# Decoded input weights of the first dense layer: kept in six SBUF slots instead of a round trip through DRAM

## The chip, the cores and the metric

The kernel runs on one core of one Trainium2 chip. The metric is the device time of one launch in microseconds (us). Three timed runs of the kernel before gave 885.88, 887.46 and 888.39 us; their median, 887.46 us, is the time that the change is measured against. The engines are called PE (TensorE, matrix products), ACT (ScalarE), DVE (VectorE), POOL (GpSimd) and SP (SyncE, which here issues every DMA). SBUF is the on-chip working memory, DRAM the memory off the core.

## The reference

Batch B = 4, sequence S = 448, 12 heads of 64, so a model width of 768. Three stages follow each other, each reading what the one before wrote:

```
attention:  scores = 0.125 * q k^T ; mix the heads with w_pre ; softmax ; mix the heads with w_post ; times v
layer one:  h = gelu_tanh(x @ w_in)           # w_in is 768 x 1024
            u, v = h[:, :512], h[:, 512:]
            v = layernorm(v) * g_ln ;  v = w_sg @ v + b_sg
            x = x + (u * v) @ w_out           # w_out is 512 x 768
layer two:  theta = x @ w_theta               # w_theta is 768 x 768
            y = w_tok_r @ (x * cos(theta)) + w_tok_i @ (x * sin(theta))
            u = x + y ;  out = u + relu(u @ w_ch)
```

The weights of the two layers are handed over as 64-bit floats. The chip turns each into a pair of 32-bit parts, a high one and a low one ("decoding"), and a product is computed as three: high by high, high by low, low by high.

## The kernel before

One program runs the three stages one after another. The order of the instructions on each engine is the order in which the Python code emits them; an engine works through its own list strictly in that order, and waits are put in where a tile is written, read or its memory used again.

**Attention** is a software pipeline over 92 steps r, each a pair of blocks of query rows. In a step SP issues the relayout of the scores of step r+4 (`blk<-s`), PE mixes the heads with w_pre for r+2 (`psB`), DVE takes the row maximum (`nmx`), ACT the exponential (`e`), POOL scales w_post (`wr`), PE mixes the heads again (`psC`), ACT and DVE write the result in two parts (`ah`, `al`), and PE multiplies by v (`psD`). Scores of a later tile (`psA`, drained by ACT into `s`) run between. The finished rows go to DRAM as `xT`.

**The decoding of w_in beside attention.** Eighteen jobs of 128 x 256 values are spread over the attention steps: all six row blocks of the right half of w_in (columns 512 to 1023, the v half), and the first three of the left half (KE = 3, the u half). A job (`decode`, L563) loads 256 KB into `draw`, lets ACT and DVE build the value, and then ACT writes the high part into a tile `dh` (`high`, L602), DVE forms the remainder, and POOL writes the low part into the same tile (`low`, L613). `dh` has one buffer there. Last, SP stores `dh` into the DRAM scratch `win_d` (`store`, L618), 256 KB. So each `dh` can be written again only after the store of the one before has landed.

**The change-over to layer one.** The last attention steps and the first units of layer one are interleaved by a small table of keys (`tail` in `moe1`): at key -7 layer one's pools are opened in the memory that early attention tiles have left, and SP issues, for k = 0 to 5, two loads of `xraw` (a 448-column and a 64-column piece of `xT`) and then `load_win(k, 1)`, which brings 512 KB of decoded w_in back from `win_d` into SBUF (`load_pair`, L647). At keys 1 to 3 follow three more, `load_win(k, 0)`. ACT and DVE split each `xraw` in two parts (`x`, L547 and L550). The unit `v_chunk` multiplies 128 rows of x by the v half: for each k three products, 18 in all (`ps<-win,x`, L554). Four v_chunks are placed into attention's tail; `psD` groups of attention stand between them. The six jobs for the rest of the u half (k = 3 to 5) are decoded there too, straight into tiles of the `win` pool. Then four `u_half` units follow, and the rest of the layer.

**Layer two** needs w_theta, which layer one decodes into the DRAM scratch `wth_d`. After layer one's last u_half the `win` pool is closed and a pool `th` opened over it; twelve loads `load_wth(k, half)` (L647) fill it, placed after the units that follow.

Of the kernel before, what the change touches and what calls it, by code (L numbers as in the profile page):

```python
# [6 lines left out]
F32 = mybir.dt.float32  # L7
F32R = mybir.dt.float32r
# [10 lines left out]
DM = H * D  # L19
# [453 lines left out]
DFF = 1024  # L473
HF = DFF // 2
KD, KF = DM // 128, HF // 128
# [7 lines left out]
KE = 3  # L483
# [7 lines left out]
class Dense:  # L491


    def __init__(self, tc, nc, io, xT, x2T, outT):
        self.tc, self.nc, self.io = tc, nc, io
        self.xT, self.x2T, self.outT = xT, x2T, outT
        self.pools, self.psum = {}, None
        self.units, self.before, self.after, self.at = [], {}, {}, 0
        self.jobs, self.job_at = [], 0
        self.raw_bufs, self.mid_bufs, self.out_bufs = 1, 1, 1  # L500
        self.const = {}


    def unit(self, fn, *a):
# [50 lines left out]

    def scratch(self, dram):
        t = lambda name, r, c: dram.tile([2, r, c], F32, name=name)
        self.win_d = t("win_d", DM, DFF)
        self.wth_d = t("wth_d", DM, DM)
        self.wtok_d = t("wtok_d", 2 * S, S)  # L560
        self.wch_d = t("wch_d", 128 * KC, DM)

    def decode(self, src, n, dst, tiles=None):  # L563

# [86 lines left out]
def moe1(d, left, right):  # L651

    tc, nc, io = d.tc, d.nc, d.io
    win_es, tail_es, tail_ps = ExitStack(), ExitStack(), ExitStack()
    win, wsg, wout, xt, uT, vraw, mv, vn, mixed, gt, res = ({} for _ in range(11))
    small = {}

    def start():
        d.open("c", 1, right, "right")
        d.open("x", 1, right, "right")  # L660
        d.open("win", 1, win_es, "right")
        for name, bufs in (("st", 4), ("v", 4), ("s", 2), ("dec", 1)):
            d.open(name, bufs, tail_es, "right")
        d.open_psum(2, tail_ps, "right")
        d.raw_bufs, d.mid_bufs, d.out_bufs = 3, 4, 4
        c = d.pools["c"]
        for name in ("eps", "hpi"):
            d.const[name] = c.tile([128, 1], F32, name=name)
        d.const["sin"] = c.tile([128, 1], F32, name="sin")
        d.const["ident"] = c.tile([128, 128], F32, name="ident")  # L670
        pair = lambda pool, n, tag: [d.pools[pool].tile([128, n], F32R, tag=f"{tag}_{i}", name=tag) for i in range(2)]
        for k in range(KE, KD):
            def tiles(k=k):
                win[k, 0] = pair("win", HF, f"win{k}_0")
                return win[k, 0]
            d.jobs += d.decode_tiles(io["w_in"], slice(128 * k, 128 * k + 128), 0, HF, tiles)
        d.jobs += [None]
        for k in range(KF):
            def tiles(k=k):
                wout[k] = pair("w", DM, f"wout{k}")  # L680
                return wout[k]
            d.jobs += d.decode_tiles(io["w_out"], slice(128 * k, 128 * k + 128), 0, DM, tiles)
        d.jobs += (d.decode_all(io["w_theta"], 0, DM, d.wth_d)
                   + d.decode_all(io["w_tok"], 0, S, d.wtok_d)
                   + d.decode_all(io["w_ch"], 0, DM, d.wch_d, 128 * KC))
# [18 lines left out]
    def rest2():  # L704
        tail_es.close()
        for name, bufs in (("st", 4), ("s", 2), ("v", 4), ("g", 1)):
            d.open(name, bufs, left)

    def load_win(k, half):
        win[k, half] = d.load_pair(d.pools["win"], d.win_d, slice(128 * k, 128 * k + 128),  # L710
                                   slice(HF * half, HF * half + HF), f"win{k}_{half}")

    def load_wsg(c):
        raw = d.stage(S, "wsgraw")
# [151 lines left out]
    for b in range(B + 1):  # L866
# [13 lines left out]
        if b < B:  # L880
            g0[b] = len(d.units)
            for f in range(KF):
                i = U(gate, b, f)
# [8 lines left out]
    for b in range(B):  # L892
# [4 lines left out]
        for c in range(nv):  # L897
# [3 lines left out]
            i = o0[b - 1][0] + late_u + c  # L901
            d.post(i, norm, b, c)
            d.post(i, norm_split, b, c)
        if b + 1 < B:
            i = u0[b] + KF
# [25 lines left out]
    def at(s, fn, *a):  # L931
        tail.setdefault(s, []).append(lambda: fn(*a))
    at(-7, start)
    for k in range(KD):
        at(-7, load_x, 0, k, "st" if k < 4 else "v")
        at(-7, load_win, k, 1)
        at(-4 + k // 2, split_x, 0, k)
    at(-3, consts)
    for k in range(KE):
        at(1 + k, load_win, k, 0)  # L940
    for key in (-4, -3, -2, -2, -1, -1, 0, 1, 2, 3, 4):
        at(key, d.tick)
    for c in range(4):
# [7 lines left out]
def moe2(d, left, win_es, last_u, m1_left):  # L951
    tc, nc, io = d.tc, d.nc, d.io
    wth, wch, wtok, z, x2, st, ut, res = ({} for _ in range(8))
    th_es = ExitStack()

    def start():
        win_es.close()
        d.open("th", 1, th_es, "right")
        d.open("xp", 2, th_es, "right")

    def load_wth(k, half):
        wth[k, half] = d.load_pair(d.pools["th"], d.wth_d, slice(128 * k, 128 * k + 128),
                                   slice(384 * half, 384 * half + 384), f"wth{k}_{half}")

    def rest():
        while d.job_at < len(d.jobs) + LAGS[0][1]:
# [183 lines left out]
    first = len(d.units)  # L1150

    d.post(last_u, start)
    for k in range(KD):
        for half in range(2):
            d.post(last_u + 1 + k, load_wth, k, half)
# [36 lines left out]
    for j, kh in enumerate(words):  # L1192
        i = tok0 - 1 + (3 * j + 1) // 2
# [21 lines left out]
def build(tc, nc, io, out):  # L1215
    with tc.manual_schedule(), ExitStack() as top:
        dram = top.enter_context(tc.tile_pool(name="scratch", bufs=1, space=bass.MemoryType.DRAM))
        xT = dram.tile([DM, B * S], F32, name="xT")
        x2T = dram.tile([DM, B * S], F32, name="x2T")
        d = Dense(tc, nc, io, xT, x2T, out)  # L1220
        d.scratch(dram)
        right, left1, left2 = ExitStack(), ExitStack(), ExitStack()
        tail, win_es, last_u, end = moe1(d, left1, right)
        th_es = moe2(d, left2, win_es, last_u, left1)
        for i in range(4):
            tail.setdefault(-2 + 2 * i, []).append(d.step)
        jobs = d.decode_all(io["w_in"], HF, DFF, d.win_d)
        jobs += d.decode_all(io["w_in"], 0, HF, d.win_d, 128 * KE)
        attention(tc, nc, io, xT, B, jobs, tail)
        while d.at < len(d.units):  # L1230
            d.step()
        th_es.close()
        right.close()
        left2.close()


# [72 lines left out]
```

## Time and profile before

| | us |
|---|---|
| timed runs, median of three | 887.46 |
| the profiled execution | 892.93 |
| its span (first to last instruction) | 891.2 |
| PE busy in the span | 854.0 (96%) |
| attention, until layer one's first product | 0 to 367 |
| change-over with attention's last products | 367 to 387 |
| layer one and layer two | 387 to 891 |

Every duration in this document comes from one profiled execution of 892.93 us, 5.47 us above the median of the timed runs. A busy share is to be read by stage: PE is busy almost without a gap in the two layers, and in attention and the change-over it waits now and then. The rows in the section before the prediction show the waits that the change touches.

### The profile page before, as it was taken

The page shows a single profiled execution, that of the slowest core. Times are in us where ns is not written, and L with a number is a line of the kernel's source. Part 1 is how long each engine was busy: PE and PEld are TensorE (multiplying, and loading weights), DVE is VectorE, ACT ScalarE, POOL GpSimd, SP SyncE. Part 2 cuts the span into 40 slices and gives each one's busy share as a digit, 9 for nine tenths or more (in the row PEclk, how much of TensorE's full clock was granted, in tenths as well). Part 3 has the DMA queues.
Part 4 walks back from the last instruction along what each step waited for, and adds up shares of the span by engine and source line. Part 5 has one row for each costly group of instructions (what it writes and reads, how often), then busy time and mean ns, then how long its engine had stood idle before and what let it go on. Part 6 is the DMA issues. An engine that isn't in the chain of part 4 may idle for free.

```text
span 891.2 us, 29399 instructions
## 1 busy us (share of the span) xinstructions
PE 854.0 (96%) x12008; PEld 673.9 (76%) x12008; DVE 660.7 (74%) x1471; ACT 535.3 (60%) x1202; POOL 253.9 (28%) x453
## 2 busy tenths in 40 slices
PE   8899999999998999799999999998999999999998
PEld 2456556565665566589898989898989999999997
DVE  3887888788888888579999998969886358338221
ACT  5888789878897887466665767427535136016010
POOL 0272254225422642000000000016607228406421
PEclk9999999999999999899999999999999999999999
DMA  6567656675676545873385857997620311300301
GB/s 203 193 210 220 212 176 213 207 230 175 217 229 201 186 168 141 270 239 98 111 280 172 279 182 234 294 348 248 212 92 29 114 34 39 114 22 7 105 20 63
DMA packets 116343, 151.15 MB, mean 170 GB/s; under 512 B 26224, under 2 KB 100208, under 8 KB 116208
## 3 DMA queue, kind: packets, MB, share of 16 engines
q1 hardware_dynamic: 116208, 149.26, 52.8%
q8 instruction: 95, 1.56, 0.8%
q14 instruction: 40, 0.33, 0.1%
HBM read 78.38 MB, written 32.31 MB: 124 GB/s over the span
## 4 chain that ended last, share of the span: by engine, by line
PE 67%; DVE 9%; DMA 8%; ACT 6%; POOL 5%; issue 4%; SPq 1%; ACTq 0%; POOLq 0%; DVEq 0%
PE ps L554 46%; PE psC L302 6%; PE psB L244 5%; PE psA L219 4%; PE psD L354 4%; ACT e L258 2%; POOL vl L197 2%; ACT s L225 2%; DVE nmx L250 1%; DMA win_d<-dh 1%; POOL vraw L188 1%; DMA blk<-s 1%; POOL wr L280 1%; DMA xres<-xT 1%; ACT ah L325 1%
## 5 line engine op out<-in xcount | busy, mean ns | idle before, releaser
L258 ACT ACTIVATE e<-psB,nmx 128x448 f32<-128x448 f32 x180 | 113.1, 637 | 32.8 <-DVE nmx L250 31.6
L331 DVE SCALAR_TENSOR_TENSOR al<-psC,ah 128x480 f16<-128x480 f32 x180 | 116.3, 647 | 9.7 <-ACT ah L325 8.8
L250 DVE TENSOR_REDUCE nmx<-psB 128x1 f32<-128x448 f32 x180 | 103.9, 618 | 16.2 <-PE psB L244 13.9
L302 PE MATMUL psC<-wr,e 64*64 64x60 f32 x5632 | 106.4, 222 | 4.3 <-issue 1.9
L550 POOL TENSOR_TENSOR x2s<-x,x2s 128x384 fp32r<-128x384 f32 x28 | 28.8, 1049 | 284.8 <-ACT x2s L547 284.8
L244 PE MATMUL psB<-blk,kpre 64*64 64x448 f32 x720 | 104.0, 546 | 4.8 <-ACT e L258 3.9
L302 PEld LDWEIGHTS psC<-wr,e 64*64 64x64 f32 x5632 | 93.7, 135 | 17.0 <-POOL wr L280 7.5
L554 PE MATMUL ps<-wtok,z 128*128 128x448 f32 x504 | 104.8, 368 | 0.0
L219 PE MATMUL psA<-k,q 64*64 64x448 f32 (+2 forms) x768 | 96.5, 551 | 7.8 <-ACT s L225 5.6
L554 PEld LDWEIGHTS ps<-wtok,z 128*128 128x128 f32 x504 | 94.6, 188 | 9.5
L354 PEld LDWEIGHTS <-vh 128*64 128x64 f16 x1536 | 57.5, 112 | 58.0 <-issue 57.8
L325 ACT ACTIVATE ah<-psC 128x480 f16<-128x480 f32 x180 | 93.7, 581 | 10.3 <-PE psC L302 10.2
L554 PE MATMUL ps<-wth,x2s 128*128 128x384 f32 x504 | 93.0, 338 | 3.2 <-POOL x2s L550 2.1
L225 ACT ACTIVATE s<-psA 124x896 f32<-124x896 f32 (+1 forms) x90 | 84.2, 936 | 12.3 <-PE psA L219 7.6
L554 PEld LDWEIGHTS ps<-wth,x2s 128*128 128x128 f32 x504 | 87.1, 188 | 4.9 <-POOL x2s L550 3.0
L554 PE MATMUL ps<-u,wch 128*128 128x448 f32 x432 | 89.9, 368 | 0.0
L554 PEld LDWEIGHTS ps<-u,wch 128*128 128x128 f32 x432 | 81.1, 188 | 8.1
L550 POOL TENSOR_TENSOR z<-zz,z 128x384 fp32r<-128x384 f32 x56 | 64.4, 1170 | 55.7 <-ACT z L547 55.6
L244 PEld LDWEIGHTS psB<-blk,kpre 64*64 64x64 f32 x720 | 37.6, 132 | 50.0 <-ACT e L258 23.8
L547 ACT ACTIVATE u<-xres 128x448 fp32r<-128x448 f32 x24 | 13.8, 577 | 99.1 <-DVE xres L1123 99.1
L264 POOL TENSOR_SCALAR rc<-sum 128x2 f32<-128x2 f32 (+1 forms) x92 | 22.4, 244 | 176.1 <-ACT e L258 175.0
L280 POOL TENSOR_SCALAR wr<-w,rc 128x60 f32<-128x60 f32 x180 | 54.5, 317 | 53.3 <-DVE rc L269 43.0
(129 smaller groups left out, 1614.5 us busy)
## 6 DMA issues: line engine op xcount, KB each, us to landing
blk<-s SPq DMA_DIRECT2D x176, 210.0 KB
draw<-in_w_in SPq DMA_DIRECT2D x24, 256.0 KB
k<-in_kvT SPq DMA_DIRECT2D x24, 224.0 KB
xraw<-xT SPq DMA_DIRECT2D x24, 224.0 KB
xres<-xT SPq DMA_DIRECT2D x24, 224.0 KB
x2T<-xres SPq DMA_DIRECT2D x24, 224.0 KB
xres<-x2T SPq DMA_DIRECT2D x24, 224.0 KB
out<-uu SPq DMA_DIRECT2D x24, 224.0 KB
```

The lines of the kernel that those rows point to most:

```text
L219: nc.tensor.matmul(ps[e][r, :S], q[p, o + r.start:o + r.stop], k[p], start=True, stop=True)
L225: nc.scalar.activation(out=out, in_=pair[:m, :, :S], func=AF.Copy, scale=0.125)
L244: nc.tensor.matmul(ps[e][c:c + 64, :S], kpre[k, e], blk[k], start=True, stop=True)
L250: nc.vector.tensor_reduce(out=nmx[r][:, e:e + 1], in_=ps[:, :S], axis=AX.X, op=ALU.max, negate=True)
L258: nc.scalar.activation(out=x, in_=ps[:, :S], func=AF.Exp, bias=m[:, e:e + 1], accum_out=sm[:, e:e + 1])
L280: nc.gpsimd.tensor_scalar(out=w, in0=wts[n], scalar1=rc[:, e:e + 1], scalar2=0.0, op0=ALU.mult, op1=ALU.add)
L302: nc.tensor.matmul(pc[r][h][c:c + 64, jc, :, SQ * e:SQ * e + SQ], x[p, c:c + 64], wr[r][e][p], start=(e == 0 and jc == 0), stop=(e == 1 an ...
L325: nc.scalar.activation(out=at_view(r, e, at[b, t][0]), in_=at_src(r, e), func=AF.Copy, scale=2.0 ** -17)
L331: nc.vector.scalar_tensor_tensor(out=al, in0=at_src(r, e), scalar=2.0 ** -17, in1=ah, op0=ALU.mult, op1=ALU.subtract)
L354: nc.tensor.matmul(ps[p, o:o + n], v[:, jc, p], a[:, i0:i0 + n], start=(o == 0 and m == 0), stop=(o > TI and m == len(terms) - 1))
L550: eng.tensor_tensor(out=out, in0=in_, in1=hi.bitcast(F32), op=ALU.subtract)
L554: self.nc.tensor.matmul(ps, l, r, start=(i == 0), stop=(i == len(terms) - 1))
```

## The change

A pool `slot` is opened before attention and stays open to the end: six tiles of 128 x 3 x 512 values, 36 KB of each partition's memory. A half row block of w_in takes two pieces of 512 values, high and low, so the eighteen pieces hold the nine half blocks that are decoded beside attention. ACT's `high` and POOL's `low` write into the pieces, and the `v_chunk` and `u_half` products read them there. Gone are `win_d`, its 18 stores of 256 KB (4.7 MB) in attention, the nine loads of 512 KB (4.7 MB) in the change-over, and the tile `dh` of attention. The `win` pool keeps the three half blocks k = 3 to 5 of the u half. The `th` pool is gone: layer two's w_theta parts for k go into slot k, both halves into one tile, with loads of the same size at the same places as before. In layer one the pools `v` and `st` change places in memory.

```diff
+    def open_slots(self, es):
+        self.open("slot", 1, es, "right")
+        self.slots = [self.pools["slot"].tile([128, 3, 512], F32R, tag=f"slot{i}", name="slot") for i in range(6)]
+    def piece(self, i):
+        return self.slots[i // 3][:, i % 3]
+    def pieces(self, k, half):
+        i = 2 * k if half else 2 * (KD + k)
+        return self.piece(i), self.piece(i + 1)
...
-        for name, bufs in (("st", 4), ("v", 4), ("s", 2), ("dec", 1)):
+        for name, bufs in (("v", 4), ("st", 4), ("s", 2), ("dec", 1)):
...
+        for k in range(KD):
+            win[k, 1] = d.pieces(k, 1)
+            if k < KE:
+                win[k, 0] = d.pieces(k, 0)
...
         at(-7, load_x, 0, k, "st" if k < 4 else "v")
-        at(-7, load_win, k, 1)
         at(-4 + k // 2, split_x, 0, k)
...
-    for k in range(KE):
-        at(1 + k, load_win, k, 0)
...
     def load_wth(k, half):
-        wth[k, half] = d.load_pair(d.pools["th"], d.wth_d, slice(128 * k, 128 * k + 128),
-                                   slice(384 * half, 384 * half + 384), f"wth{k}_{half}")
+        if half == 0:
+            wth[k] = d.pools["slot"].tile([128, 2, 2, 384], F32R, tag=f"slot{k}", name="wth")
+        t = wth[k][:, half]
+        nc.sync.dma_start(out=t.bitcast(F32), in_=d.wth_d[:, 128 * k:128 * k + 128, 384 * half:384 * half + 384]
...
-        jobs = d.decode_all(io["w_in"], HF, DFF, d.win_d)
-        jobs += d.decode_all(io["w_in"], 0, HF, d.win_d, 128 * KE)
+        for half, ks in ((1, range(KD)), (0, range(KE))):
+            for k in ks:
+                jobs += d.decode_tiles(io["w_in"], slice(128 * k, 128 * k + 128), HF * half, HF * half + HF,
+                                       lambda k=k, half=half: d.pieces(k, half))
```

The instructions of PE, ACT, DVE and POOL stay the same ones in the same order; what changes is the tile that some of them name, and what they wait for. SP's list gets shorter by 27 DMAs.

**SP, the change-over.** `DMAHW0` to `DMAHW7` are the semaphores that DMAs raise in turn. Before, from the last store of attention's rows that precedes layer one's loads:

```order
L367 DMA xT<-x 128x3x120 [waits DMAHW0_49,DVE_49]
L737 DMA xraw<-xT 128x448 [waits DMAHW1_49]
L739 DMA xraw<-xT 128x64 [waits DMAHW2_49]
L647 DMA win_1_8986<-win_d 128x2x512 [waits DMAHW3_49]
L737 DMA xraw<-xT 128x448 [waits DMAHW4_49]
L739 DMA xraw<-xT 128x64 [waits DMAHW5_49]
L647 DMA win_1_8991<-win_d 128x2x512 [waits DMAHW6_49]
L737 DMA xraw<-xT 128x448 [waits DMAHW7_49]
L739 DMA xraw<-xT 128x64 [waits DMAHW0_49]
L647 DMA win_1_8996<-win_d 128x2x512 [waits DMAHW1_49]
```

and now:

```order
L367 DMA xT<-x 128x3x120 [waits DVE_49]
L747 DMA xraw<-xT 128x448 [waits DMAHW7_49]
L749 DMA xraw<-xT 128x64 [waits DMAHW0_49]
L747 DMA xraw<-xT 128x448 [waits DMAHW1_49]
L749 DMA xraw<-xT 128x64 [waits DMAHW2_49]
L747 DMA xraw<-xT 128x448 [waits DMAHW3_49]
L749 DMA xraw<-xT 128x64 [waits DMAHW4_49]
L747 DMA xraw<-xT 128x448 [waits DMAHW5_49]
```

The loads of x stand one behind another, where each pair was followed by 512 KB of weights.

**ACT in attention, one decode step.** `dp` and `dl` are the words of a job, `dh` or `slot` takes its high part. Before:

```order
L586 ACTIVATE dp<-draw 128x256 [waits DMAHW6_49,Pool_49]
L587 ACTIVATE dl<-draw 128x256
L258 ACTIVATE e,sum<-psB,nmx 128x448 [waits DVE_49,Activation_49] x2
L325 ACTIVATE ah<-psC 128x48x10 [waits PE_49] x2
L225 ACTIVATE s<-psA 124x896 [waits PE_49]
L602 ACTIVATE dh<-da 128x256 [waits DMAHW6_49,DVE_49]
L258 ACTIVATE e,sum<-psB,nmx 128x448 [waits DVE_49,Activation_49] x2
```

and now:

```order
L596 ACTIVATE dp<-draw 128x256 [waits DMAHW5_49,Pool_49]
L597 ACTIVATE dl<-draw 128x256
L258 ACTIVATE e,sum<-psB,nmx 128x448 [waits DVE_49,Activation_49] x2
L325 ACTIVATE ah<-psC 128x48x10 [waits PE_49] x2
L225 ACTIVATE s<-psA 124x896 [waits PE_49]
L612 ACTIVATE slot<-da 128x256 [waits DVE_49]
L258 ACTIVATE e,sum<-psB,nmx 128x448 [waits DVE_49,Activation_49] x2
```

The write of the high part no longer waits for a DMA; in the 17 later jobs of the 18 it did.

**SP in attention, around one store of a job.** `blk` is a relayout buffer. Before:

```order
L236 DMA blk_131<-s 120x1x448 [waits DMAHW1_49,PE_49]
L618 DMA win_d<-dh 128x2x256 [waits DMAHW2_49,Pool_49]
L236 DMA blk_132<-s 120x1x448 [waits DMAHW3_49,PE_49]
L236 DMA blk_133<-s 120x1x448 [waits DMAHW4_49]
L236 DMA blk_134<-s 120x1x448 [waits DMAHW5_49,PE_49]
```

and now:

```order
L236 DMA blk_139<-s 120x1x448 [waits DMAHW7_49,PE_49]
L236 DMA blk_140<-s 120x1x448 [waits DMAHW0_49,PE_49]
L236 DMA blk_141<-s 120x1x448 [waits DMAHW1_49]
L236 DMA blk_142<-s 120x1x448 [waits DMAHW3_49,DMAHW2_49,PE_49]
```

The store is gone, and every DMA behind it raises another of the eight semaphores than before; a relayout here and there names two of them.

## Rows read from the trace of the kernel before

**Rows 1.** The page's first part: busy time, share of the span, instructions.

```profile
PE 854.0 (96%) x12008; PEld 673.9 (76%) x12008; DVE 660.7 (74%) x1471; ACT 535.3 (60%) x1202; POOL 253.9 (28%) x453
```

**Rows 2.** Chain of waits, change-over: start us, us, what.

```profile
363.12 7.34 DMA xraw<-xT
...
370.48 5.59 DMA win<-win_d
...
376.20 1.62 PE ps L554 x3
377.82 2.78 PE psD L354 x60
...
385.67 1.53 PE psD L354 x72
```

**Rows 3.** By windows: stretch, busy of five engines, granted clock, DMA share, GB/s.

```profile
364.00:367.00 3.00, 1.95 (x53) 1.73 (x52) 1.14 (x2) 0.51 (x2) 0.00 (x0) 1.00 0.95 310
...
370.00:373.00 3.00, 1.92 (x6) 1.26 (x6) 1.60 (x5) 1.25 (x3) 0.00 (x0) 0.81 1.00 327
373.00:376.00 3.00, 2.23 (x5) 0.83 (x3) 1.32 (x3) 1.01 (x2) 0.00 (x0) 0.50 1.00 335
```

**Rows 4.** Timeline of PE, change-over; in brackets idle before, and its releaser.

```profile
366.84 0.24 PE L354 MATMUL psD<-al,vh 128*64 128x120 f16 x2 [1.05 <-issue]
...
367.07 1.75 PE L554 MATMUL ps<-win,x 128*128 128x512 f32 x6
369.98 0.93 PE L554 MATMUL ps<-win,x 128*128 128x512 f32 x3 [1.16 <-DMA win<-win_d]
```

**Rows 5.** Timeline of SP's queue, change-over.

```profile
355.60 2.21 SPq L737 DMA_DIRECT2D xraw<-xT  x1
...
360.19 0.47 SPq L737 DMA_DIRECT2D xraw<-xT  x1
...
369.86 0.32 SPq L739 DMA_DIRECT2D xraw<-xT  x1
```

**Rows 6.** Timeline of ACT, change-over: the splits of x, first and last.

```profile
363.64 0.62 ACT L547 ACTIVATE x<-xraw 128x512 fp32r<-128x512 f32 x1
...
374.73 0.63 ACT L547 ACTIVATE x<-xraw 128x512 fp32r<-128x512 f32 x1 [1.34 <-DMA xraw<-xT]
```

**Rows 7.** Timeline of PE behind the change-over.

```profile
395.42 14.75 PE L554 MATMUL ps<-x,win 128*128 128x448 f32 x72
```

**Rows 8.** Timeline of ACT: the last decode of w_in.

```profile
392.03 0.41 ACT L602 ACTIVATE win<-da 128x256 fp32r<-128x256 f32 x1
```

**Rows 9.** Chain of waits, first wait for a store in attention.

```profile
86.62 5.02 DMA win_d<-dh
```

**Rows 10.** Timeline of ACT around that wait.

```profile
88.08 0.96 ACT L225 ACTIVATE s<-psA 124x896 f32<-124x896 f32 x1
91.72 0.42 ACT L602 ACTIVATE dh<-da 128x256 fp32r<-128x256 f32 x1 [2.68 <-DVE vmx L154]
```

**Rows 11.** Timeline of PE, the w_pre products around it.

```profile
83.98 0.93 PE L244 MATMUL psB<-blk,kpre 64*64 64x448 f32 x8
87.33 1.01 PE L244 MATMUL psB<-blk,kpre 64*64 64x448 f32 x8
...
96.82 0.55 PE L244 MATMUL psB<-blk,kpre 64*64 64x448 f32 x4
```

**Rows 12.** Timeline of ACT, second wait for a store.

```profile
272.30 0.42 ACT L602 ACTIVATE dh<-da 128x256 fp32r<-128x256 f32 x1 [2.31 <-DMA win_d<-dh]
```

**Rows 13.** Chain of waits, the longest relayout in attention.

```profile
158.81 5.70 DMA blk<-s
```

**Rows 14.** Timeline of SP's queue, end of layer one.

```profile
566.43 4.00 SPq L647 DMA_DIRECT2D wth<-wth_d  x6
```

**Rows 15.** Timeline of PE, layer one's last u_half units.

```profile
543.75 14.76 PE L554 MATMUL ps<-x,win 128*128 128x448 f32 x72
```

More of the change, by code (lines that the diff above doesn't have):

```diff
@@ L500, in __init__ @@
         self.raw_bufs, self.mid_bufs, self.out_bufs = 1, 1, 1
-        self.const = {}
+        self.const, self.slots = {}, []
     def unit(self, fn, *a):
@@ L557, in scratch @@
         t = lambda name, r, c: dram.tile([2, r, c], F32, name=name)
-        self.win_d = t("win_d", DM, DFF)
         self.wth_d = t("wth_d", DM, DM)
@@ L707, in rest2 @@
             d.open(name, bufs, left)
-    def load_win(k, half):
-        win[k, half] = d.load_pair(d.pools["win"], d.win_d, slice(128 * k, 128 * k + 128),
-                                   slice(HF * half, HF * half + HF), f"win{k}_{half}")
     def load_wsg(c):
@@ L957, in start @@
         win_es.close()
-        d.open("th", 1, th_es, "right")
         d.open("xp", 2, th_es, "right")
     def load_wth(k, half):
-        wth[k, half] = d.load_pair(d.pools["th"], d.wth_d, slice(128 * k, 128 * k + 128),
-                                   slice(384 * half, 384 * half + 384), f"wth{k}_{half}")
+        if half == 0:
+            wth[k] = d.pools["slot"].tile([128, 2, 2, 384], F32R, tag=f"slot{k}", name="wth")
+        t = wth[k][:, half]
+        nc.sync.dma_start(out=t.bitcast(F32), in_=d.wth_d[:, 128 * k:128 * k + 128, 384 * half:384 * half + 384]
+                                                   .rearrange("i p c -> p i c"))
+        wth[k, half] = t[:, 0], t[:, 1]
     def rest():
@@ L1226, in build @@
             tail.setdefault(-2 + 2 * i, []).append(d.step)
-        jobs = d.decode_all(io["w_in"], HF, DFF, d.win_d)
-        jobs += d.decode_all(io["w_in"], 0, HF, d.win_d, 128 * KE)
+        slots = top.enter_context(ExitStack())
+        d.open_slots(slots)
+        jobs = []
+        for half, ks in ((1, range(KD)), (0, range(KE))):
+            for k in ks:
+                jobs += d.decode_tiles(io["w_in"], slice(128 * k, 128 * k + 128), HF * half, HF * half + HF,
+                                       lambda k=k, half=half: d.pieces(k, half))
         attention(tc, nc, io, xT, B, jobs, tail)
@@ L1233, in build @@
         right.close()
+        slots.close()
         left2.close()
```

## The prediction

> **What bounds the kernel now.** I read four views in this order. The page's first part shows that PE is busy for 96% of the span [rows 1]; the rest, 37 us, is all that waits can give back directly, and a lowered clock hides more inside the busy time. The chain of waits then tells where something else than PE sets the end. In the two layers it runs along PE's products nearly throughout, so a stage that is begun earlier should end earlier by as much. Between attention and layer one it leaves PE: one load of x for 7.34 us, then one load of decoded w_in for 5.59 us, and only then PE's products [rows 2]. Third, the windows by engine over that stretch: the DMA engines are full (share 0.95 to 1.00, 310 to 335 GB/s), PE is busy for about two thirds, and its granted clock goes from 1.00 to 0.81 to 0.50, so from 2.4 to 1.2 GHz [rows 3]. Fourth, the timelines of ACT inside attention, where twice a decode step stands still because the tile `dh` has not yet been stored [rows 9 to 12].
>
> So two places are touched that are on the path (the change-over, and the `dh` waits), and a third, the DMA traffic beside attention, that is on it only now and then.
>
> **The change part by part.**
>
> *A, the change-over.* Nine loads of 512 KB go; six of them stood between the loads of x. The bytes asked for before layer one's first v_chunk is complete fall from 6 x (512 + 256) KB = 4.7 MB to 1.6 MB. Before, the first v_chunk begins at 367.07, right behind attention's products, and ends at 376.20 + 1.62 = 377.82 [rows 2, 4]. Its first six products, which had their data, took 1.75 us [rows 4], so all 18 take 3 x 1.75 = 5.25 us without waits: it would end at 372.32, 5.5 us sooner. What is late next? Not the weights, which are then in SBUF since attention. The loads of x: the first issue takes 2.21 us from 355.60, later ones about 0.47 [rows 5]; twelve in a row are issued by about 363. The last one of before was used 4.9 us after its issue, under full queues [rows 5, 6]; even so late, the last piece is there at 368. ACT is free for the first split at 363.64 [rows 6], and six splits at 0.62 us, with DVE's behind them and attention's own rows between, are over at about 369.5 by my estimate (3.7 us of ACT, 0.7 of DVE behind the last, 1.5 for attention's). The sixth block of x is wanted at 367.07 + 5 x 0.88 = 371.4. So PE itself is the next limit, and the whole 5.5 us count. Then the attention group behind it: 60 products took 2.78 us at the low clock, 72 of the later group 1.53 us [rows 2], so 1.25 us more if the clock has not fallen. A is 6.75 us.
>
> The low clock in this stretch follows PE's waits for DMA: 1.00 while attention's products run out, 0.81 and then 0.50 while the first v_chunk gets its blocks one at a time [rows 3]. The Trainium skill, "TensorE: Matmul & The Clock Gate", section "HAM oscillation — how this bites in real kernels", says that products which wait for a DMA between small groups make the clock fall again each time. The trace agrees, with 0.50 at 373 to 376. By that rule the gain in clock comes only if the remaining loads of x leave no such gaps; that is a rival below.
>
> Bounds of A: upwards 6.75 + 1.05, as the gap of 1.05 us in attention's last products, put down to instruction issue, lies in the full DMA stretch [rows 4] and may go too: 7.8 us. Downwards 1.0 us, if the clock falls as before: eighteen products at 1.62 per three [rows 2] are 9.72 us against 5.25, 4.5 us given back, and the 1.25 us too. I take 6.75: the work to be done has its inputs in time even at the latencies of before.
>
> Does it last? The u_half units begin at 395.42, without a gap [rows 7]; what they need last is the decode whose high part ACT writes at 392.03 [rows 8]. In ACT's list that stands behind the gelu of a v_chunk, so it moves forward with PE, and its loads find an emptier queue. The three loads at keys 1 to 3 were hidden behind PE's work and count nothing.
>
> *B, the waits for `dh`.* ACT's write of the high part waited in 17 of 18 jobs for the store before it. In most it had landed. Twice not: the store issued at 86.62 took 5.02 us to land [rows 9], and ACT, done with its row before at 89.04, began at 91.72, 2.68 us idle [rows 10]. The row names DVE, but the store's end at 91.64 is what lies just before the start, and the chain has it. The second stood still for 2.31 us [rows 12]. Behind it on ACT were the exponentials that PE's next step needs: PE's w_pre groups came 3.35 us apart before the first wait, and the next two steps took 9.49 instead of 6.70, 2.8 us lost [rows 11]. So an idle ACT passes through to PE in full. Sum 4.99 us. Bounds: 0, if another wait stands there at once, and 5.6 (2 x 2.8). I take 5.0, nearest to the ACT rows.
>
> *C, traffic and SP's queue in attention.* Eighteen stores of 256 KB go, with their issues on SP. No engine waited for those issues on its own. A store ahead in the queues costs what is behind it 256 KB at 310 to 335 GB/s [rows 3], 0.8 us. The longest relayout on the chain, 5.70 us [rows 13], would so be shorter by 0.8. I take 1.0 us of gain for all of attention. Bounds: 5.7 gained, if that wait vanishes; 5.4 lost, if two waits of the size of B arise elsewhere, since every DMA now raises another semaphore and the relayouts land at other times.
>
> *Edits at nothing.* ACT's and POOL's decode instructions write the same shapes to another address. The six w_theta slots: the first loads were issued at 566.43 [rows 14], while the last u_half product had ended at 558.50 [rows 15], so the wait for slots 4 and 5 is long over, and slots 0 to 3, read by v_chunks, are free before. If that cover were gone, the loads would be held for as long as PE is late, which nothing in the order suggests. Pools `v` and `st` swapped: no load of x got a wait for an engine.
>
> *Sum.* 892.93 - 6.75 - 5.0 - 1.0 = 880.2 us for the profiled execution. It is 5.47 us longer than the median; I carry the difference over: 887.46 - 12.75 = 874.7, forecast **875 us**.
>
> **The rivals.**
>
> *R1: attention gives its part back.* The waits for `dh` vanish, but the steps then stand still for something else (the next load of k or v, POOL's scaling), and only A counts: 887.46 - 6.75 = 880.7. For it: attention has many small waits, and both B waits lie near loads of v rows. Against it: ACT's row before had ended, and only the store's landing lies between it and the next [rows 9, 10].
>
> *R2: the relief in attention is larger.* The 5.70 us relayout wait [rows 13] and its lowered clock go with the traffic: C becomes 5.7 or more, 874.7 - 4.7 = 870.0, or 868 with the rest of the bounds. For it: the DMA engines are busy for most of attention. Against it: the relayouts are themselves most of that traffic, and stay.
>
> *R3: the clock falls all the same.* The loads of x, still one by one, make PE wait between the blocks of the first v_chunk, and it runs at 1.2 GHz as before: A is 1.0, so 887.46 - 7.0 = 880.5. Against it: the times worked out above leave 1.9 us of slack for the last block.
>
> *R4: slower.* The place is SP's queue in attention. Each DMA waits for the semaphore that an earlier one raises, and SP is strictly in order; with the stores out, relayouts come to wait for other, larger loads, and everything behind them waits too. Price: 2.8 us of PE per event, as in B [rows 11]. It turns the sum from six events on (12.75 / 2.8 = 4.6 to break even, one more to be seen): six give 891.5 for 92 steps. For it: a few relayouts now name two such semaphores. Against it: there is less in the queues at each point, not more.
>
> That the change doesn't do what it says can be left out: the loads and stores are gone from SP's list.
>
> **How the numbers follow.** Forecast (870 to 880): 0.60. R1 0.18, R2 0.12, R3 0.06, R4 0.04. About 0.3%, or 2.7 us, is what a measurement of this kernel can tell from no change, so faster is below 884.8 and slower above 890.1. The forecast, R2, and nearly all of R1 and R3 lie below 884.8; of these two I leave 0.04 in between. Faster 0.92, same 0.05, slower 0.03. The range, 867 to 883 us, reaches from R2 with A's upper bound to above R1 and R3, and leaves R4 and the tails out.
>
> **What the profile after would show.** For A: no `win<-win_d`, the first v_chunk's 18 products in 5 to 6 us with no idle put down to a load, granted clock 1.00 through the change-over, and from the last attention group to the end the same length as before. For B: ACT's high-part row directly behind its row before, and w_pre groups 3.3 to 3.4 us apart there. For C: a shorter or absent relayout on the chain. I am wrong on A if ACT's or DVE's splits of x, not PE, are what the first v_chunk waits for; on B if attention ends less than 4 us earlier than before; on the whole if layer one or two gets longer by what was won, above all around the loads of w_theta.

## The result, and the profile after

The changed kernel takes 880.17 us (median of 18 runs), the kernel before 888.53 us (18 runs beside it). The ratio is 0.9897, with a 95% interval of 0.9880 to 0.9915: some 9 us faster, where 12.75 us were forecast. One of the 18 runs, 890.64 us, was over 1.5% longer than the fastest of its kernel and is left out of the ratio. Two later sets gave 0.9885 [0.9859, 0.9911] and 0.9879 [0.9856, 0.9901], so 9 to 11 us over the three. Durations from here on come from several profiled executions; each place says of which kernel, and the first profile of each is meant where nothing else is said.

The page's first part of the changed kernel, to set beside [rows 1]. PE has the same number of instructions and is busy for 6.3 us less; the span fell from 891.2 to 880.9 us. How much of the gain is busy time, where a lowered clock makes products longer, this pair alone doesn't tell: two later profiles of before (below) have 848.2 and 850.9 us busy, two of the changed kernel 847.9 and 847.4. Over three profiles each, the span differs by 10.4 us and the busy time by 3.4.

```profile
PE 847.7 (96%) x12008; PEld 672.5 (76%) x12008; DVE 659.0 (75%) x1471; ACT 534.7 (61%) x1202; POOL 253.4 (29%) x453
```

The chain of waits at the change-over, to set beside [rows 2]: start, us, what.

```profile
357.94 2.73 DMA xraw<-xT
...
364.47 1.38 PE psD L354 x48
365.85 4.39 PE ps L554 x18
370.24 1.53 PE psD L354 x72
371.77 4.39 PE ps L554 x18
376.17 1.53 PE psD L354 x72
```

Where before two transfers of 7.34 and 5.59 us stood, PE now goes from attention's last products (`psD`) into the first v_chunk (`ps`, 18 products) without a break. One load of x, 2.73 us, is still on the chain ahead of that; PE's own wait there, for DVE, is 0.38 us. The windows [rows 3] and the timeline of PE [rows 4] say the same: PE is busy throughout at a granted clock of 1.00, and the DMA share falls from the second of these stretches on.

```profile
365.00:368.00 3.00, 3.00 (x44) 2.51 (x39) 3.00 (x9) 2.55 (x6) 0.00 (x0) 1.00 0.93 281
368.00:371.00 3.00, 3.00 (x52) 2.31 (x52) 2.18 (x7) 2.78 (x6) 0.00 (x0) 1.00 0.62 207
371.00:374.00 3.00, 3.00 (x50) 2.53 (x45) 2.90 (x9) 2.22 (x7) 0.93 (x2) 1.00 0.35 100
```

```profile
365.78 4.46 PE L554 MATMUL ps<-slot,x 128*128 128x512 f32 x18
371.70 4.46 PE L554 MATMUL ps<-slot,x 128*128 128x512 f32 x18
377.63 8.66 PE L554 MATMUL ps<-slot,x 128*128 128x512 f32 x36
```

x is split well ahead. These are ACT's rows, beside [rows 6]: four splits run in one piece from 363.10, and the sixth begins at 366.39, after a wait of 0.20 us.

```profile
363.10 2.19 ACT L547 ACTIVATE x<-xraw 128x512 fp32r<-128x512 f32 x4
...
366.39 0.63 ACT L547 ACTIVATE x<-xraw 128x512 fp32r<-128x512 f32 x1 [0.20 <-DMA xraw<-xT]
```

I measure the change-over from the start of the first v_chunk to that of the third: 377.63 - 365.78 = 11.85 us. In before the first starts at 367.07 [rows 4] and the third at 387.13, so 20.06 us. These are the second and the third of before (with the fourth), and the window in which the second begins:

```profile
380.53 5.14 PE L554 MATMUL ps<-win,x 128*128 128x512 f32 x18
387.13 8.45 PE L554 MATMUL ps<-win,x 128*128 128x512 f32 x36
```

```profile
378.00:382.00 4.00, 4.00 (x76) 3.61 (x73) 2.72 (x9) 3.97 (x9) 0.93 (x2) 0.50 0.40 132
```

**8.2 us of the span's 10.3 were won there.** PE's waits for `win` in that stretch of before were 3.2 us (3.7 and 4.4 in its later profiles); the rest is products that took longer. Behind it nothing changed: from the third v_chunk to the end are 503.3 us, 504.1 before.

In attention the `dh` waits [rows 9 to 12] are gone. ACT's decode row follows its row before directly (beside [rows 10]):

```profile
91.15 0.97 ACT L225 ACTIVATE s<-psA 124x896 f32<-124x896 f32 x1
91.95 0.48 ACT L612 ACTIVATE slot<-da 128x256 fp32r<-128x256 f32 x1
```

And yet attention ends only 1.3 us earlier (365.78 against 367.07). PE's timeline shows what stands there instead, beside [rows 11]: the w_pre groups come 3.35 to 3.55 us apart (3.3 to 3.4 were forecast), and then PE waits for 1.75 us put down to "issue", which is a wait for nothing that the profile shows.

```profile
87.07 0.93 PE L244 MATMUL psB<-blk,kpre 64*64 64x448 f32 x8
90.42 1.01 PE L244 MATMUL psB<-blk,kpre 64*64 64x448 f32 x8
93.97 1.27 PE L244 MATMUL psB<-blk,kpre 64*64 64x448 f32 x8
...
99.07 0.52 PE L302 MATMUL psC<-wr,e 64*64 64x60 f32 x21 [1.75 <-issue]
```

PE's waits from 20 to 366 us, grouped (us in total, times, longest), have one row that is far larger than before, where the same group came to 1.9 us:

```profile
PE psC L302 <- issue: 9.1, 9, 2.4
```

So two readings were open. Theory 1: the gain is the change-over; the `dh` waits were worth next to nothing, since attention has other stalls, which differ from execution to execution. Theory 2: the `dh` waits are worth their 5 us, and the change has brought new stalls which take them back.

### The profile page after: what moved, and what is told of

Read it like the earlier page. It is cut to its first block, busy times and chain, and to the rows that moved or that the text cites. A ratio compares the mean times of both kernels' runs of the same rounds, so it can differ in the third digit from the quotient of the medians.

```text
span 880.9 us, 29335 instructions
## 1 busy us (share of the span) xinstructions
PE 847.7 (96%) x12008; PEld 672.5 (76%) x12008; DVE 659.0 (75%) x1471; ACT 534.7 (61%) x1202; POOL 253.4 (29%) x453
## 4 chain that ended last, share of the span: by engine, by line
PE 70%; DVE 11%; ACT 5%; DMA 5%; POOL 4%; issue 4%; SPq 1%; POOLq 0%; ACTq 0%; DVEq 0%
PE ps L554 47%; PE psC L302 7%; PE psB L244 5%; PE psA L219 5%; PE psD L354 5%; POOL vl L197 2%; DMA wth<-wth_d 2%; ACT e L258 1%; ACT s L225 1%; DVE nmx L250 1%; DMA blk<-s 1%; DVE al L331 1%; POOL wr L280 1%; DMA xres<-xT 1%; POOL vraw L188 1%
## 5 line engine op out<-in xcount | busy, mean ns | idle before, releaser
L219 PE MATMUL psA<-k,q 64*64 64x448 f32 (+2 forms) x768 | 94.4, 545 | 6.2 <-ACT s L225 5.2
```

The costliest lines, as they stand in the source:

```text
L219: nc.tensor.matmul(ps[e][r, :S], q[p, o + r.start:o + r.stop], k[p], start=True, stop=True)
```

## The experiments

**One part alone: two `dh` tiles in the kernel before.**

```diff
-        self.raw_bufs, self.mid_bufs, self.out_bufs = 1, 1, 1
+        self.raw_bufs, self.mid_bufs, self.out_bufs = 1, 1, 2
```

> The kernel before with one line changed: attention's decode gets two `dh` tiles instead of one; stores, loads and change-over stay. Theory 1 (the two `dh` waits are worth next to nothing in the median, since other stalls in attention take their place; the gain of the change is the change-over alone): 0 to 1.5 us faster than before, ratio 0.998 to 1.000, although the trace no longer has `dh <-DMA win_d` among ACT's waits. Theory 2 (the waits cost their 5.0 us in every execution, and the changed kernel lost that again by something it brought itself): 4 to 6 us faster, ratio 0.993 to 0.9955.

> The kernel before with two `dh` tiles in attention, a second time with as many rounds, since the first interval of 0.9984 to 1.0028 is wide. Theory 1: ratio 0.997 to 1.001 again. Theory 2: 0.993 to 0.9955.

Measured: ratio 1.0006 [0.9984, 1.0028], and in the second set 0.9999 [0.9984, 1.0013]. ACT's waits for `dh` are gone from both traces, and it gains nothing; 5 us would be 0.9944. PE's timeline shows what became of one of them. This is the stretch of the first `dh` wait in the kernel before, and then in the one with two `dh` tiles, between the same two products (`psA` of one step, `psV` of a later one); these are all PE's waits in it.

```profile
77.24 0.98 PE L219 MATMUL psA<-k,q 64*64 64x448 f32 x8 [0.62 <-ACT s L225]
92.81 1.59 PE L244 MATMUL psB<-blk,kpre 64*64 64x448 f32 x8 [1.68 <-ACT e L258]
108.44 0.38 PE L165 MATMUL psV<-ident,vmj 128*6 128x128 f32 x2 [0.21 <-ACT s L225]
```

```profile
78.53 0.98 PE L219 MATMUL psA<-k,q 64*64 64x448 f32 x8 [0.62 <-ACT s L225]
94.64 1.17 PE L302 MATMUL psC<-wr,e 64*64 64x60 f32 x61 [0.40 <-POOL wr L280]
99.92 0.26 PE L302 MATMUL psC<-wr,e 64*64 64x60 f32 x1 [0.41 <-issue]
106.38 1.13 PE L294 MATMUL psC<-wr,e 128*128 128x96 f32 x8 [0.39 <-POOL wr L280]
109.58 0.38 PE L165 MATMUL psV<-ident,vmj 128*6 128x128 f32 x2 [0.21 <-ACT s L225]
```

The stretch lasts 31.20 us in the one and 31.05 in the other. The 1.68 us that PE waited for ACT's exponential are gone, and 1.20 us of waits for POOL's `wr` and for issue have come. It is one pair of profiles: in the two others of before the stretch lasts 31.12 and 31.03 us, and in the second with two tiles 33.55, with an issue wait of 2.08 us in it.

**Are the stalls the same in every execution?** The kernels before and after, unchanged.

> The changed kernel once more, unchanged, for another profiled execution. Theory 1 (the stalls of attention differ from execution to execution): ratio 0.988 to 0.992 again, but the waits of PE at L302 put down to issue come to another sum than 9.1 us, at other times of the span, and the time of the first v_chunk differs from 365.78 us by over 0.5 us. Theory 2 (the change itself placed them): 8 to 10 us again, at the same places, the 2.40 us one near 182.7 us among them.

> The kernel before once more, unchanged, for a second profiled execution (the first, at 892.93 us, was over 5 us above the median of 887.7). Theory 1 (the two `dh` waits of 2.7 and 2.3 us were those of that one execution, and are no part of the median): the `dh` waits of ACT in attention come to under 2.5 us in sum, at other places, and the first v_chunk starts at 361 to 364 us instead of 367.07. Theory 2 (they are in every execution and something else makes up for them): 4 to 6 us of `dh` waits again.

> The kernel before a third time, for a third profiled execution. As for the second: theory 1 forecasts under 2.5 us of `dh` waits and another sum of PE's issue waits than 3.9 us; theory 2 forecasts 4 to 6 us of `dh` waits. In both, the length from the first to the third v_chunk is 19 to 21 us, as in the first profile (20.1).

> The changed kernel, unchanged, beside the three others on the same chip: ratio 0.988 to 0.9915, as in the two sets before. In its trace, PE's waits put down to issue in attention come to another sum than 9.1 and 3.0 us if they differ by execution, and the first v_chunk's start moves with them.

Measured: the changed kernel 0.9885 and 0.9879 as above; the two single runs of before 886.37 and 887.62 us. From all profiles of one kind (us; issue: PE's waits put down to issue up to the first v_chunk; psB: PE's wait there for ACT's exponentials):

```
profile of                 dh waits of ACT   psB   issue   first v_chunk   first to third   span
before                           5.5         3.2    3.9       367.07           20.06        891.2
before, second                   6.8         2.7    3.2       362.04           18.78        884.6
before, third                    5.4         2.8    4.4       361.87           20.20        885.8
before, two dh                   0           0      3.8       362.42           19.61        886.3
before, two dh, second           0           0      7.5       365.91           17.69        887.6
after                            0           0      9.1       365.78           11.85        880.9
after, second                    0           0      3.0       359.67           11.86        876.6
after, third                     0           0.2    1.7       358.13           11.86        872.9
```

Half of theory 1 falls: the `dh` waits are in every execution of before (5.4 to 6.8 us), not a matter of the first. These are ACT's rows of the third, and PE's:

```profile
ACT dh L602 <- DVE dp L604: 2.8, 1, 2.8
ACT dh L602 <- DMA win_d<-dh: 2.6, 2, 2.4
```

```profile
PE psB L244 <- ACT e L258: 2.8, 3, 1.4
```

So half of what ACT waits reaches PE, about 2.8 us, and the run with two tiles says that of this nothing measurable reaches the end. The other half holds: the issue waits come to 9.1, 3.0 and 1.7 us in three executions of one program, and the first v_chunk's start follows them almost us for us (365.78, 359.67, 358.13: each less its issue waits is 356.4 to 356.7). Theory 2 falls too: the change did not bring them. This is the third execution's row; 0.7 us before a `psA` product makes up its 1.7:

```profile
PE psC L302 <- issue: 1.0, 3, 0.6
```

**The traffic of the change-over put back.** Nine transfers of 512 KB in the places of the removed loads, from DRAM to DRAM (`load_again`, cut here), for which no instruction waits; then only the six between x's loads.

```diff
...
+        at(-7, load_again, k, 1)
         at(-4 + k // 2, split_x, 0, k)
     at(-3, consts)
+    for k in range(KE):
+        at(1 + k, load_again, k, 0)
```

> The changed kernel, and at the nine places where w_in's parts were loaded again (six between x's loads, three later) a transfer of 512 KB runs on the same queue, from w_in's words in DRAM to a DRAM scratch that nobody reads; no instruction waits for it. Theory 1 (the change-over is slow because its transfers share the queue's bandwidth, and that is 8.2 us): most is given back, 6 to 9 us slower than the changed kernel, ratio to before 0.997 to 1.001, with x's splits waiting for xraw and a DMA share of 0.9 to 1.0 around the first v_chunks. Theory 2 (the change-over is worth 3 to 4 us and the rest is from the `dh` waits): ratio 0.993 to 0.995. Rival (products waited for win itself, not for bytes; x's lead hides the extra transfers): at most 2 us back, ratio 0.990 to 0.992.

> The changed kernel with only the six transfers of 512 KB between x's loads put back (DRAM to DRAM, nobody waits for them), not the three later. If the first v_chunk's place in the queue is what costs: nearly all that nine took is lost, 6 to 8.5 us against the changed kernel, ratio to before 0.996 to 0.999. If the cost goes by bytes: two thirds of what nine took (8.7 us), 5 to 6.5 us, ratio 0.994 to 0.9965. If the three later ones cost most (they delay the decode of the last parts of w_in, for whose DVE steps attention's last products waited in the run with nine): under 4 us, ratio under 0.9935.

Measured: with nine 0.9981 [0.9958, 1.0004], 0.96% or 8.5 us above the changed kernel in the same set; with six 0.9981 [0.9957, 1.0005]. So traffic of that size, put back there, costs most of what the change gained, and the six between x's loads cost it alone as far as the intervals tell (the profiled run with six, 880.01 us, was the shortest of its twelve, median 884.98). By bytes, six would cost two thirds of nine's 0.96%. That is 0.9949 counted from the 0.9885 of the changed kernel, which lies outside the interval of the six, and 0.9975 counted from the 0.9911 of the last experiment's kernel in the same set, which lies inside; so that is not excluded.

But the waits of before don't come back by it, since the products don't read these transfers. From the first to the third v_chunk the profile with nine has 16.48 us and that with six 13.57, where the changed kernel has 11.86 and before 18.8 to 20.2 (17.7 once with two `dh` tiles):

```profile
367.74 3.77 PE L554 MATMUL ps<-slot,x 128*128 128x512 f32 x15
...
384.22 9.42 PE L554 MATMUL ps<-slot,x 128*128 128x512 f32 x36
```

```profile
361.49 4.88 PE L554 MATMUL ps<-slot,x 128*128 128x512 f32 x18
375.06 8.66 PE L554 MATMUL ps<-slot,x 128*128 128x512 f32 x36
```

So these two runs price traffic at that place; they don't show that the removed loads cost as much, or in the same way. In the run with nine, DMA is full and the clock falls to 0.50, already under attention's last products:

```profile
358.00:362.00 4.00, 1.69 (x65) 1.38 (x66) 2.36 (x5) 1.20 (x4) 0.54 (x2) 1.00 0.94 281
362.00:365.00 3.00, 3.00 (x66) 2.73 (x59) 1.46 (x3) 2.06 (x5) 0.00 (x0) 0.50 1.06 383
```

There PE had stood still for 2.31 us, put down to issue; and behind the second v_chunk attention's last group waits for DVE, which is held by decode steps whose load came late (the last row, of the chain):

```profile
361.59 1.43 PE L302 MATMUL psC<-wr,e 64*64 64x60 f32 x52 [2.31 <-issue]
...
381.92 0.23 PE L354 MATMUL psD<-ah,vh 128*64 128x88 f16 x2 [3.02 <-DVE x L362]
```

```profile
366.69 8.01 DMA draw<-in_w_in
```

**The traffic of the stores put back or doubled.** The changed kernel with each decoded block stored from its slot (24 stores for the 18 blocks, as some lie in two slots); and the kernel before with each block stored twice. Both edits are cut to the place of the store.

```diff
...
+            if back is not None:
+                back(n)        # store of this block's slot piece(s) to a DRAM scratch
             if tiles:
                 return
...
```

```diff
...
             nc.sync.dma_start(out=dst, in_=box["hl"][:, :, :n].bitcast(F32))
+            if again is not None:
+                nc.sync.dma_start(out=again, in_=box["hl"][:, :, :n].bitcast(F32))
...
```

> The changed kernel, and each decoded half block in a slot is also stored to a DRAM scratch that nobody reads (18 blocks of 256 KB, 24 stores, from the slots, so no tile waits for a store). Theory 1: the stores run beside attention and cost 0 to 1 us, so the ratio to before stays at 0.989 to 0.991. Rival (the traffic of the stores, the term C, was worth more than the 1.0 us forecast): 2 to 5 us are given back, ratio 0.992 to 0.996.

> The changed kernel with the 18 blocks also stored to DRAM, a second time, beside the changed kernel on the same chip. If the stores' traffic costs nothing: within 0.1% of the changed kernel's ratio in this same set. If it is worth 2 to 3 us (0.9923 against 0.9885 in the first set): 0.2 to 0.4% above it again.

> The kernel before, and each of the 18 blocks decoded in attention is stored a second time, to another DRAM scratch that nobody reads; the one `dh` tile is free only when both stores have landed. Theory 1 (ACT has slack beside attention's PE: of 5.0 to 6.8 us of `dh` waits only the 2.7 to 3.2 us of PE's waits `psB <-ACT e` reach PE, and they take the place of other waits there): the `dh` waits grow to 10 us or more, the time by 0 to 3 us, ratio 1.000 to 1.0035. Theory 2 (each us of a `dh` wait is a us of the end): as much again as before, 5 to 7 us slower, ratio 1.0055 to 1.008.

Measured: stores put back, 0.9923 [0.9895, 0.9952] beside 0.9885 of the changed kernel in that set, and 0.9905 [0.9880, 0.9931] beside 0.9879. Twice 0.26 to 0.38% up, 2.3 to 3.4 us; each pair of intervals overlaps, but the sign came twice, and the mean times of the six runs differ by 2.8 and 2.4 us with a standard error of about 1.1 in each set. The two profiles don't show it (the first v_chunk at 359.35 and 362.13, within the spread of the table). Stores doubled: 1.0061 [1.0040, 1.0082], 5.4 us slower. That is the time that theory 2 gave, but not for its reason: the `dh` waits did not grow to 10 us, as theory 1 had it for this run and theory 2 needs, they came to 5.8, no more than in before.

```profile
ACT dh L603 <- DMA again_d<-dh: 3.6, 3, 2.2
ACT dh L603 <- DVE al L331: 2.2, 1, 2.2
```

So 18 more stores cost 5.4 us with no longer `dh` waits. What a store costs is not the tile that it holds. It may be its traffic beside attention or its place in SP's list, ahead of relayouts and loads; no run separates the two. In which waits of PE that traffic ends, one profile each doesn't tell. One hint goes through all fourteen: a product `psA` at 161 to 168 us waits for ACT's `s` for 0.57 to 1.14 us in the six profiles without the stores (four times 0.57), and for 0.57 to 2.87 us, 1.34 in the mean, in the eight with them.

**The order of two pools.** The changed kernel with `st` opened ahead of `v` again.

```diff
-        for name, bufs in (("v", 4), ("st", 4), ("s", 2), ("dec", 1)):
+        for name, bufs in (("st", 4), ("v", 4), ("s", 2), ("dec", 1)):
```

> The changed kernel with the two pools `v` and `st` opened in the old order, so x's first four raw tiles lie where they lay before. Theory 1 (the gain is the transfers', the order of the pools is worth nothing): ratio to before 0.987 to 0.992, like the changed kernel. Rival (the swap is what brings x's first loads forward): x's first load waits on SP 2 us longer or more, and 2 to 5 us are given back, ratio 0.992 to 0.996.

Measured: 0.9911 [0.9878, 0.9944], and first to third v_chunk 11.86 us as with the swap. It is worth nothing that shows.

## Why the prediction was right, and where not

*Direction and range.* Faster, and 880.17 lies within 867 to 883. The gain is 9 us (11 at most, over the sets) instead of 12.75, and it is made up differently. The range was drawn to hold R1 and R3 too, so the number alone doesn't choose: 880.17 lies just outside the 870 to 880 that had the chance of 0.60, beside R1's 880.7. In part the hit is luck: the 5.0 us of B did not come, and A and C, both forecast too low, made up for some of them.

*A, the change-over: the mechanism was right, the size a little low.* Forecast 6.75 us; the first pair of profiles has 8.2, and the mean of the five with the old change-over in the table less 11.86 is 7.4 (5.8 to 8.3). The changed kernel with the stores put back measures it by time: it lacks only what the stores' absence gives, and it is 0.77% and 0.95% faster than before, 6.8 and 8.4 us, of which next to nothing is B. Each step was seen: no `win<-win_d`, no wait of PE for x's splits, clock 1.00. The Trainium skill, "TensorE: Matmul & The Clock Gate", section "HAM oscillation — how this bites in real kernels", has the clock fall again when products wait for a DMA between small groups; the trace agrees, with no such wait left and the clock at 1.00. Two terms were short, and they are the 1.5 us between 6.75 and 8.2. The 18 products take 4.46 us, not 5.25: I had taken three times the first six of before, of which 1.75 us is not the pace of a long group. And the second v_chunk, which I put at nothing, took 5.14 us in before, where its first 1.5 us lie in a stretch at a clock of 0.50, and takes 4.46 now. The issue gap of 1.05 us, which I kept for the upper bound of 7.8, lies ahead of the first v_chunk and so outside these 8.2. The rival R3 (the clock falls all the same) is out.

*B, the waits for `dh`: this step failed.* "So an idle ACT passes through to PE in full" is what fell. Alone it is worth 0.0% [-0.16, +0.13], so at most 1.4 us of the forecast 5.0. PE's own wait there was 1.68 us [rows 11 give 2.8 for two steps], already less than ACT's 2.68, and in the stretch shown, what PE no longer waits for ACT it waits for POOL's `wr` and at "issue". This is rival R1, for B alone. I had argued from the one row on ACT; I should have asked in PE's rows what is late next.

*C, traffic: too low.* Forecast 1.0 us for the eighteen stores; 2.3 to 3.4 by putting them back, and 5.4 for a second eighteen. R2 held that a relief in attention beyond B exists, and by these estimates it does, but of about half its size. The sign set for it, a shorter or absent relayout on the chain, says nothing: the longest one from 20 us on is 5.62 us in the changed kernel (5.70 before), 7.29 in its second profile, and there is none in its third, nor in the second and third of before.

```profile
250.25 5.62 DMA blk<-s
```

*The sum.* With the nine transfers' 8.5 us for A, the runs give 8.5 + 0 + 2.3 to 3.4 = 10.8 to 11.9 us, a little over the 9.1, 10.2 and 10.7 measured as wholes.

*My own sign for B was a poor one.* "Wrong on B if attention ends less than 4 us earlier": it ended 1.3 us earlier in the first profile, and 7.4 us in the second one of the same kernel. The end of attention moves by 7.6 us among three executions of one program, so no single pair of profiles can judge 5 us there. The first profile of before was a late one too, with 367.07 where two others have 362; its time, 892.93, was 5.47 us over the median, which I carried along as a constant. A part of it is one stall: these windows of before hold the 5.70 us relayout [rows 13], PE's wait of 1.87 us behind it (1.00 and 0.57 in the other two profiles), and a lowered clock.

```profile
150.00:160.00 10.00, 10.00 (x316) 6.70 (x312) 9.06 (x22) 9.77 (x25) 3.09 (x10) 1.00 0.85 277
160.00:170.00 10.00, 8.13 (x212) 5.27 (x212) 6.13 (x15) 7.40 (x18) 1.99 (x8) 0.85 0.70 206
```

*Edits at nothing, and R4.* Right. Layer two's first loads of w_theta are issued at 556.61 (SP's timeline, beside [rows 14]), 8.0 us after the last product that reads a slot (546.63 + 1.97), and SP's w_theta loads show no wait for an engine. SP's first load of x still takes 2.34 us (2.21 in [rows 5]); a row of the kind that R4 needs, a relayout held by another load, comes to 0.2 us in either kernel.

```profile
556.61 4.03 SPq L971 DMA_DIRECT2D wth<-wth_d  x6
```

## What to carry to other kernels

Transfers that stand between the inputs of a stage and the engine that waits for them can cost twice: here 3.2 to 4.4 us as waits, and 2.6 to 5.0 as products that ran longer, at a lowered clock. The timelines of that stretch gave the forecast within 1.5 us; what it missed was the low clock in the unit behind. A wait of an engine beside the critical one is priced in the critical engine's rows, by what is late next there. And before a term of 5 us is taken from one profile, look at how far that profile lies from the median: here by 5.47 us, as much as the term.

## What was not expected of the hardware

PE's waits put down to issue go with its instruction stream. In the page's table of DMA queues (packets, MB, share of 16 engines) one is of kind instruction, with as many packets in both kernels, 16 KB each, counted on the same 16 engines as the data:

```profile
q1 hardware_dynamic: 108864, 139.82, 50.1%
q8 instruction: 95, 1.56, 0.7%
```

In the fourteen profiles, from 20 us to the first v_chunk, 45 of these waits are longer than 0.6 us, up to 2.86. Each ends 2.2 to 3.3 us after the beginning of one such packet. Two of them, in the changed kernel (packet at 182.4) and in the run with six transfers (packet at 352.5):

```profile
185.06 0.38 PE L302 MATMUL psC<-wr,e 64*64 64x60 f32 x9 [2.40 <-issue]
```

```profile
354.69 0.52 PE L302 MATMUL psC<-wr,e 64*64 64x60 f32 x21 [2.86 <-issue]
```

The place is sharper still. Counted along PE's own rows (weight loads, products and semaphore rows, by start), all 84 waits put down to issue in these stretches, small ones too, stand at the same point, within one row, of a step of 256 rows; and 95 packets for 24,016 weight loads and products is one for 253. So these waits stand where PE's list passes into another packet's worth. That PE waits there for instructions which arrive late follows from time and place; no run changed the stream to test it. Most of the 73 packets up to the first v_chunk bring no wait, and the same step differs: that of the 2.40 us wait cost 2.12, 1.84, 1.57, 1.30 and 0.74 us in five other profiles, and is not among the longer waits of the rest. Data traffic alone doesn't set it: with the stores put back, these waits were 0.9 us in one profile and 6.0 in the other. What makes them differ from execution to execution stays open.

The second thing is the granted clock. With six transfers put back it fell under attention's own products, to 0.70 and 0.50, after PE had been idle for more than half of a stretch, and the third stretch ran at half speed without any idle:

```profile
350.00:354.00 4.00, 1.83 (x40) 0.98 (x37) 2.36 (x5) 1.75 (x4) 1.12 (x4) 1.00 0.91 273
354.00:358.00 4.00, 3.31 (x81) 3.08 (x80) 1.70 (x3) 2.30 (x5) 0.00 (x0) 0.70 1.06 386
358.00:362.00 4.00, 4.00 (x54) 3.66 (x54) 2.81 (x8) 2.04 (x4) 0.00 (x0) 0.50 0.99 253
```
